# Queries and keys of a pair of heads split together on 128 rows: per-row scales from the pair's own tiles, operands put in place by transfers inside SBUF

## The chip, the cores and the metric

The kernel runs on one core of one Trainium2 chip. The metric is the device time of one execution in microseconds (us), the median of the runs shown. The core has a matrix engine (PE; PEld in the profile is its weight load), a vector engine (DVE), an activation engine (ACT), GpSimd (POOL), and SP, which here issues every transfer (DMA).

## The reference

Attention with a decay bias, and behind it a feed-forward layer on its output, all in fp32. B = 8 batches, H = 8 heads, S = 576 positions, head size 64; 4608 rows of 512 through a layer of 2048.

```python
scores = q @ k.T / sqrt(64)
cum = cumsum(max(s, 0));  bias = -(cum[:, None] - cum[None, :])
scores = where(causal, -1e6, scores + min(bias, 0))
attn = softmax(scores);  out = attn @ v
x = out.transpose(0, 2, 1, 3).reshape(4608, 512)
h = x @ w_in;  g = where(h > 0, h, exp(min(h, 0)) - 1)
result = g @ w_out
```

The weights come as 64-bit floats and are decoded to fp32 on the chip.

## The kernel before

**A plan orders everything.** The program lists its operations, each with a priority, the engines that could do it and a cost in ns for each (class Plan, from L86 on). The planner goes through them by the earliest possible start and then by priority, chooses the engine where there is a choice, and fixes each engine's order. On the chip each engine goes through its own order and waits where data is missing. So a change of one operation can move many others, on every engine. PE gets matmuls on a scratch bank (L1501) where the plan has nothing for it at the start.

**Pieces.** The work on attention goes by pairs of heads (four pairs a batch). First come the *low pairs*: the first 320 positions of batches 0 to 3, 16 pairs, computed with fp32 matmuls (prepare_low, scoring_low, weighing_low; tiles kl, ql, vs, products avl and trl). Then the *main pairs*: batches 4 to 7 whole (a short block of 64 positions of both heads, whose names carry None, and then each head with four blocks of 128 rows), and the late rows of batches 0 to 3 (each head with two blocks): 32 main pairs. A unit of these is prepared (prepare), scored (scoring: matmuls, a custom DVE step, L1053, exp on ACT, L1058), normalised, transposed by SP (L389, tiles T<-p, 192 times) and multiplied by the values (weighing, L1212).

The feed-forward layer goes by chunks of rows. The first chunk is *native*, in fp32 straight on the decoded weights (L1377 first layer, L1431 second). The 17 *main* chunks work on splits: every fp32 factor is scaled by a power of two, rounded to fp16 (the high part; `scaled`, whose ways are POOL L408, ACT L409, DVE L410), and the remainder is a second fp16 number. Three matmuls then stand for one (L1381, L1438).

**Weights.** load_unit brings a piece of a weight (tile raws), decodes it (ACT L675, DVE L679 and L684) and takes its peak (L606 on DVE or L609 on ACT). weight_scales (through scales_of: L629 on DVE, PE `flat` L640, DVE L632 to L636, PE `every` L643, DVE L645) makes the scales from all the peaks. Then split_unit makes the 32 high parts and the 32 remainders (DVE, L699), which the main chunks need. The scale of the low pairs' values is made in the same call, as its third span:

```python
scales_of(-600, [(A_IN, NF + 1), (A_OUT, NF + 1), (A_LOW, N_CUT * NP + 1)], 0)
```

A_LOW is the range of the peaks of V of all 16 low pairs. The first main chunk takes rows of low pairs, whose scales (chunk_scales, cs) come from this call.

**Main pairs.** For each of the 8 groups (a batch, or its late rows), group_values loads the values (va), loads all q and k of the group once more into tile sx (8 loads of 288 KB a group) and takes their peaks (128 rows by 1152, L606 or L609). From them come the group's scales of v, q and k. prepare then works head by head. K and Q lie in tiles stk and stq twice, on rows 0 to 63 and 64 to 127. The high parts are made on all 128 rows (kh, qs). The q high part on 64 rows goes to tile q2 by a transfer (L384 q<-qs). The remainders are taken on 64 rows (L1008): for q in the lower rows of qs, for k in the upper rows of k2. Below them stand three rows of decay (aux). A score is two matmuls per block (L1050): qs by kh, and q2 by k2.

Of the kernel before, what the change touches and what calls it, by code (L numbers as in the profile page):

```python
# [9 lines left out]
F32 = mybir.dt.float32  # L10
# [7 lines left out]
P = 128  # L18
# [9 lines left out]
N_ST, N_A, N_AV, N_H, N_IO, N_G, N_X, N_T, N_K, N_V = 3, 2, 1, 3, 3, 1, 1, 2, 2, 4  # L28
# [307 lines left out]
def kernel(  # L336
# [178 lines left out]
    def weigher(q):  # L515

        def rows():
            t = q.v[HB:]
# [7 lines left out]
        return rows  # L526

    def ones():

        for q, k in ((q2s, k2s), *zip(q2, k2)):  # L530
            op(60, [("Pool-M", 2600.0, weigher(q))], [], [(q, "ones")])
            op(60, [("Pool-M", 400.0, lambda k=k: pool.memset(k.v[HB:], 0.0))], [], [(k, "aux")])
# [46 lines left out]

    groups = [(b, False) for b in range(N_CUT, B)] + [(b, True) for b in range(N_CUT)]  # L580
    A_LOW, A_IN, A_OUT = 0, N_CUT * NP + 1, N_CUT * NP + 1 + NF + 1
    A_GROUP = A_OUT + NF + 1
    A_EACH, N_SCALES = NP + 1 + 3 + 3, 6
    peaks = plan.buf(const, [P, A_GROUP + len(groups) * A_EACH], F32, "peaks")

    all_tops = [plan.buf(const, [P, P], F32, f"tops_{m}") for m in range(2)]
    all_ones = plan.buf(const, [P, P], F32, "all_ones")
    scales = plan.buf(const, [P, 4 + N_SCALES * len(groups)], F32, "scales")
# [14 lines left out]
    def peak(prio, n, src, reads, at, axis=mybir.AxisListType.X, aside=None, also=()):  # L603

        col = slice(at, at + 1)
        ways = [("DVE-SB", 100 + 1.04 * n, lambda: dve.tensor_reduce(  # L606
            peaks.v[:, col], src(), axis, ALU.max, apply_absolute_value=True))]
        if aside is not None:
            ways.append(("ACT", 480 + n / 1.2, lambda: act.activation(  # L609
                aside(), src(), AF.Abs, accum_out=peaks.v[:, col])))  # L610
        op(prio, ways, reads, [(peaks, at), *also])
# [131 lines left out]
    def prepare_low(u):  # L743
# [23 lines left out]
        peak(prio, n_low * D, lambda: u.vs.v, [u.vs], A_LOW + b * NP + j, mybir.AxisListType.XY,  # L767
# [840 lines left out]
```

## Time and profile before

| | |
|---|---|
| runs | 1047.59, 1048.26 (median), 1049.46 us |
| profiled execution, whole | 1049.36 us |
| its span, first to last instruction | 1047.6 us |
| granted clock of the matrix engine | 0.996 |
| PE / DVE / ACT / POOL busy | 1014.1 / 854.6 / 696.6 / 309.2 us |
| transfers | 169.26 MB, mean 162 GB/s |

Busy time leaves out waiting. In a view of the stretches of the span, busy time stands beside the length of each stretch, and the granted clock (1.00 is full) beside it. In a line of the order of time, what stands in square brackets is the idle time ahead of the instruction and who ended it. A group's line gives busy time and the mean ns of one. Line numbers of before and after differ: L1050 is L1030 in the changed kernel, L1053 is L1033, L1381 is L1370, L1377 is L1366, L1431 is L1420, L699 is L695, L645 is L641.

### The profile page before, as it was taken

To read this page: it belongs to the slowest core of one execution; us is meant where nothing else is said; L and a number is where in the kernel's file an instruction comes from. 1 tells how busy PE (TensorE), PEld (TensorE's weight loads), DVE (VectorE), ACT (ScalarE), POOL (GpSimd) and SP (SyncE) were. 2 spreads that over 40 slices of the span, in tenths; PEclk is the share of its full clock that TensorE was granted. 3 is DMA by queue.
4 is the path that set the end of the run, shared out by engine and by line. 5 is a ranking of instruction groups with operands and counts; after the bars stand their busy time and mean duration, and the time that the engine had idled before them with its cause. 6 is when DMAs were issued, how large, how long until landed. Compare 5 with 4: busy or idle time off the path is not lost.

```text
span 1047.6 us, 22165 instructions
## 1 busy us (share of the span) xinstructions
PE 1014.1 (97%) x7354; PEld 696.8 (67%) x7354; DVE 854.6 (82%) x2222; ACT 696.6 (66%) x1568; POOL 309.2 (30%) x545
## 2 busy tenths in 40 slices
PE   8879998999999999999999999999999999999998
PEld 7656764666666666666666766666666676767665
DVE  7898656988888988989998999889888888876232
ACT  4788677766776765667777766676666666765343
POOL 6343114123353332335354434123421122210000
PEclk9999999999999999999999999999999999999999
DMA  8999856458889886688758866876785856664000
GB/s 250 251 263 277 250 150 180 129 127 180 188 205 189 171 205 135 147 142 209 158 141 168 215 150 145 175 180 161 156 180 140 154 140 137 145 121 102 6 21 21
DMA packets 289843, 169.26 MB, mean 162 GB/s; under 512 B 205856, under 2 KB 263424, under 8 KB 289728
## 3 DMA queue, kind: packets, MB, share of 16 engines
q1 hardware_dynamic: 289728, 167.84, 68.6%
q8 instruction: 58, 0.95, 0.4%
q14 instruction: 57, 0.47, 0.2%
HBM read 98.99 MB, written 19.24 MB: 113 GB/s over the span
## 4 chain that ended last, share of the span: by engine, by line
PE 50%; DVE 3%; DMA 2%; issue 1%; SPq 1%; POOL 0%; ACT 0%; DVEq 0%; POOLq 0%
PE o L1438 21%; PE h L1381 20%; PE sc L1050 4%; PE av L1212 4%; DVE p L1111 1%; DMA stk<-in_kT_dram 0%; DMA T<-p 0%; DVE h L1413 0%; DVE p L1053 0%; DMA stq_None<-in_qT_dram 0%; SPq L389 0%; DMA stq<-in_qT_dram 0%; DMA q<-qs 0%; DVE qs L1008 0%; DMA xc<-x_dram 0%
## 5 line engine op out<-in xcount | busy, mean ns | idle before, releaser
L1381 PE MATMUL h<-xh,wp 128*128 128x256 f16 x2176 | 397.6, 274 | 6.0 <-DVE wp L699 3.4
L1438 PE MATMUL o<-wp,gg 128*128 128x512 f16 x1632 | 393.8, 379 | 0.0
L1381 PEld LDWEIGHTS <-wp 128*128 128x128 f16 x3264 | 318.7, 98 | 74.5 <-DVE wp L699 5.3
L1381 PE MATMUL h<-xl,wp 128*128 128x256 f16 x1088 | 297.7, 274 | 0.9 <-DVE xl L1357 0.9
L1438 PEld LDWEIGHTS <-gg 128*128 128x128 f16 x1632 | 158.3, 98 | 143.4
L1058 ACT ACTIVATE p<-p,mn 128x192 f32<-128x192 f32 (+1 forms) x224 | 139.7, 624 | 43.7 <-DVE mn L1053 40.8
L1111 DVE SCALAR_TENSOR_TENSOR p<-p,sm,p 128x512 f16<-128x512 f32 (+3 forms) x233 | 149.0, 666 | 5.5 <-ACT p L1107 4.2
L1393 ACT ACTIVATE g<-h,cs 128x512 f32<-128x512 f32 x136 | 93.1, 684 | 90.5 <-PE h L1381 89.8
L1413 DVE SCALAR_TENSOR_TENSOR h<-g,cs,h 128x512 f32<-128x512 f32 x136 | 102.0, 750 | 52.7 <-ACT g L1400 51.4
L1417 ACT ACTIVATE gg<-h 128x512 f16<-128x512 f32 x133 | 78.8, 592 | 60.9 <-DVE h L1413 57.8
L1053 DVE CUSTOM_DVE_ANT_0 p<-sc,maskw 128x192 f32<-128x192 f32 (+1 forms) x224 | 106.0, 484 | 15.4 <-PE sc L1050 10.2
L1420 DVE SCALAR_TENSOR_TENSOR gg<-h,gg 128x512 f16<-128x512 f32 x136 | 93.2, 685 | 18.2 <-ACT gg L1417 17.2
L1103 POOL TENSOR_SCALAR p<-p,sm 128x64 f16<-128x64 f32 (+3 forms) x80 | 52.3, 659 | 144.5 <-DVE sm L1064 68.5
L1107 ACT ACTIVATE p<-p,sm 128x512 f16<-128x512 f32 (+3 forms) x128 | 72.4, 588 | 18.0 <-issue 6.9
L1050 PE MATMUL sc<-kh,qs 128*128 128x192 f16 (+2 forms) x256 | 75.8, 300 | 1.3 <-DVE mn L1053 0.7
L1050 PE MATMUL sc<-k,q 128*128 128x192 f16 (+2 forms) x256 | 75.5, 299 | 0.8 <-DMA q<-qs 0.7
L1212 PEld LDWEIGHTS <-v 128*64 128x64 f16 x896 | 45.4, 110 | 20.2 <-issue 9.8
L1212 PE MATMUL av<-T,v 128*64 128x256 f16 (+5 forms) x896 | 58.6, 280 | 0.2 <-DMA T<-p 0.2
L408 POOL TENSOR_SCALAR v<-va,scales 128x320 f16<-128x320 f32 x37 | 22.4, 611 | 109.4 <-PE av L1212 91.3
L408 POOL TENSOR_SCALAR qs<-stq,scales 128x256 f16<-128x256 f32 (+1 forms) x36 | 25.2, 701 | 91.3 <-PE sc L1050 80.9
L1008 DVE SCALAR_TENSOR_TENSOR k<-stk,scales,kh 64x576 f16<-64x576 f32 x61 | 49.9, 819 | 0.5
L1400 ACT ACTIVATE g<-g 128x512 f32<-128x512 f32 x77 | 48.4, 628 | 2.0
(189 smaller groups left out, 1441.8 us busy)
## 6 DMA issues: line engine op xcount, KB each, us to landing
stk<-in_kT_dram SPq DMA_DIRECT2D x64, 288.0 KB
va<-in_vb_dram SPq DMA_DIRECT2D x32, 320.0 KB
sx<-in_qT_dram SPq DMA_DIRECT2D x32, 288.0 KB
sx<-in_kT_dram SPq DMA_DIRECT2D x32, 288.0 KB
raws<-in_w_in_dram SPq DMA_DIRECT2D x16, 512.0 KB
raws<-in_w_out_dram SPq DMA_DIRECT2D x16, 512.0 KB
out_dram<-ost SPq DMA_DIRECT2D x32, 256.0 KB
stq<-in_qT_dram SPq DMA_DIRECT2D x32, 256.0 KB
```

Of the source, the lines that this page charges most:

```text
L1050: pe_.matmul(view(sc.v[:, :cw]), l, r, start=n == 0, stop=n == len(pairs) - 1)
L1053: op(prio, [("DVE", 84 + dve_p(cw), lambda i=i, sc=sc: dve.tensor_tensor_reduce(pt.v[:, i * cw : (i + 1) * cw], sc.v[:, :cw], mv(i * cw, c ...
L1058: op(prio, [("ACT", 480 + w / 1.2, lambda: act.activation(pt.v[:, :w], pt.v[:, :w], AF.Exp, bias=mn.v[:, n - 1 : n], scale=-1.0, accum_out ...
L1107: ("ACT", 295 + n / 1.2, lambda part=part: act.activation(part(t16, 0), own(part), AF.Copy, scale=sm.v[:, r])),
L1111: ("DVE-SB", dve_2(n), lambda part=part: dve.scalar_tensor_tensor(part(t16, 1), own(part), sm.v[:, r], part(t16, 0), ALU.mult, ALU.subtract)),
L1212: pe_.matmul(av.v[w.h * HB : (w.h + 1) * HB, dst], w.values.v[:, w.h, kb, v], part(w, kb, m), start=kb == 0 and m == 0 and v == 0, stop=kb ...
L1381: pe_.matmul(columns(k), weight_part(f, 0, part)[1]()[:, c * P : (c + 1) * P], xx.v[:, c], start=(c == 0 and m == 0), stop=(c == NCB - 1 a ...
L1393: op(side, [("ACT", act_c(W) + (0 if native else 90), lambda: act.activation(g.v, hp.v, AF.Exp, scale=1.0 if native else by(3)))], [hp] + ...
L1413: op(side, [("DVE", dve_p(W), lambda: dve.scalar_tensor_tensor(hp.v, g.v, by(2 if sign[0] else 1), hp.v, ALU.mult, ALU.max))], [g, cs], [hp])
L1417: ("ACT", act_c(W), lambda: act.activation(gg.v[:, 0], hp.v, AF.Copy, scale=2.0**-DOWN)),
L1420: op(side, [("DVE", dve_p(W), lambda: dve.scalar_tensor_tensor(gg.v[:, 1], hp.v, 2.0**-DOWN, gg.v[:, 0], ALU.mult, ALU.subtract))], [hp, ( ...
L1438: pe_.matmul(acc[i].v, gg.v[:, g, at], weight_part(f, 1, part)[1](), start=(f == 0 and m == 0), stop=(f == NF - 1 and m == 2),)
```

## The change

1. *Scales.* The loads and peaks of sx are gone. group_values makes the scale of the values only. The scale of q and k is taken for each pair and for each row of its 128 (row d of one head, row d of the other): peaks over the pair's own stk and stq, and four small DVE steps (powers). A row's scale of q and that of k cancel in the product.
2. *Low values.* Each of batches 0 to 3 gets a scale of its own for its low values, made when its fourth pair's peak is there. The weights' scales are made from the weights' peaks alone.
3. *Preparing.* A pair is prepared at once: one head's K on rows 0 to 63 and the other's on rows 64 to 127 (two loads), Q the same way (two or four loads), then the high parts and the remainders of K and Q on all 128 rows of both heads, the short block included. Twelve transfers of 64 rows, from SBUF to SBUF, bring the parts to the four operands of a *set*: Q1 (high, low), Q2 (high, weights of the decay rows), K1 (high, high), K2 (low, decay rows). One more transfer brings the decay rows.
4. *Places.* There are two sets, used by turns: one in a place of its own, one in the place of w_all[1], which the decoded weights hold until they are split. va stays in w_all[0].

```diff
-    A_LOW, A_IN, A_OUT = 0, N_CUT * NP + 1, N_CUT * NP + 1 + NF + 1
+    A_LOW, A_IN, A_OUT = 0, N_CUT * (NP + 1), N_CUT * (NP + 1) + NF + 1
...
-        scales_of(-600, [(A_IN, NF + 1), (A_OUT, NF + 1), (A_LOW, N_CUT * NP + 1)], 0)
+        scales_of(-600, [(A_IN, NF + 1), (A_OUT, NF + 1)], 0)
...
+        if j == NP - 1:
+            scales_of(-600, [(A_LOW + b * (NP + 1), NP + 1)], C_LOW + b)
...
-        home = w_parts[NG - 1] if at == 0 else w_all[(at - 1) % 2]
+        home = w_parts[NG - 1] if at == 0 else w_all[0]
...
-        for kind in range(2):
-            for c in range(2):
-                sx = plan.buf(sb, [P, 2 * S], F32, f"sx_{at}_{kind}_{c}", tag="sx")
...
-                    load(prio, dst, src, [], [(sx, m)], HB * 2 * S * 4)
-                peak(prio, 2 * S, lambda sx=sx: sx.v, [], first + NP + 1 + 3 * kind + c,
-                     aside=lambda sx=sx: sx.v, also=[sx])
-        scales_of(prio, [(first, NP + 1), (first + NP + 1, 3), (first + NP + 4, 3)], col)
+        scales_of(prio, [(first, NP + 1)], col)
...
-        load(prio, lambda: u.q2.v[:HB, :w], lambda: u.qs.v[:HB, :w], [(u.qs, 0)], [(u.q2, "q")], HB * w * 2)
...
-        remainder(w, lambda: u.qs.v[low, :w], lambda: sq.v[low, :w], lambda: u.qs.v[low, :w], 0, low,
-                  [(u.qs, 0)], [sq, (u.qs, 1)])
-        remainder(n, lambda: k_own(u.k2, top), lambda: k_view(st.v[top, :n]), lambda: k_own(u.kh, top), 1, top,
-                  [u.kh], [st, (u.k2, "kl")])
...
+    def prepare_pair(u, o):
...
+        for m, rows in enumerate(HALF):
+            load(prio, lambda m=m, rows=rows: sk.v[rows, :n], lambda m=m: kT[b, :HB, 2 * j + m, :n], [], [(sk, m)],
+                 HB * n * 4)
...
+        peak(prio, w, lambda: sq.v[:, :w], [sq], 0, aside=lambda: unread(w), dst=pk)
+        peak(prio, n, lambda: sk.v[:, :n], [sk], 1, aside=lambda: unread(n), dst=pk)
...
+        op(prio, [("DVE-SB", 350.0, powers)], [(pk, 0), (pk, 1)], [(pk, 2)])
...
+            scaled(prio, size, high, x, lambda: by(m), [src, (pk, 2)], [(t, 0)])
...
+                ("DVE-SB", dve_2(size), lambda: dve.scalar_tensor_tensor(
+                    low(), x(), by(m), high(), ALU.mult, ALU.subtract)),
...
+        split(1, n, kp, sk)
+        split(0, w, qp, sq)
...
+                load(prio, dst, lambda own=own: src.v[own, part, :size], [(src, part)], [(o, (label, h))], HB * size * 2)
...
+        spread(kp, 0, n, top, K1, "kh")
+        spread(kp, 0, n, low, K1, "kh2")
+        spread(qp, 0, w, top, Q1, "qh")
+        spread(qp, 0, w, top, Q2, "qh2")
...
+        spread(kp, 1, n, top, K2, "kl")
+        spread(qp, 1, w, low, Q1, "ql")
```

What this does to the order is seen on three engines. On PE before, at the end of the low pairs: `flat` and `every` are the two small matmuls of the weights' scales (the third column of `every` is the low values), sc_3_4_0 is the last score of the last low pair, o is the native chunk, h<-xh the first main matmul.

```order
L640 MATMUL flat_2034<-ident,tops_145 128x128
L849 MATMUL avl_2_1994<-tl_2_1988,vs_103 64x192 x2
L834 MATMUL trl_2_2_2043<-ident,p_84 128x128
L834 MATMUL trl_2_2_2043<-ident,pl_3_2_1832 128x128
L1431 MATMUL o_1_1385<-wa_1514,gg_7_1928 128x512
L643 MATMUL every_2048<-own_2038,all_ones 128x3
L849 MATMUL avl_2_1994<-tl_2_1988,vs_103 64x64 x2
L1050 MATMUL sc_3_4_0_2055<-kl_3_1717,ql_3_1836 128x320
L1381 LDWEIGHTS wp_2057
L1381 MATMUL h_0_2108<-xh,wp_2057 128x256
```

On PE now, at the first of the low pairs of the last batch (sc_0): the two small matmuls of the weights' scales.

```order
L1420 MATMUL o_0_1318<-wa_700,gg_2_1501 128x512
L636 MATMUL flat_1621<-ident,tops_145 128x128
L847 MATMUL avl_3_1596<-tl_3_1591,vs_122 64x256 x2
L832 MATMUL trl_3_1_1631<-ident,p_87 128x128
L832 MATMUL trl_3_1_1631<-ident,p_180 128x128
L832 MATMUL trl_3_1_1631<-ident,pl_2_3_1384 128x128
L832 MATMUL trl_3_1_1631<-ident,pl_2_3_1397 128x128
L1420 MATMUL o_0_1318<-wa_700,gg_2_1501 128x512
L639 MATMUL every_1643<-own_1626,all_ones 128x2
L847 MATMUL avl_3_1596<-tl_3_1591,vs_122 64x192 x2
L1030 MATMUL sc_0_3_0_1649<-kl_0_1236,ql_0_1299 128x320
```

They stand two columns wide among the native chunk, three low pairs and most of a fourth ahead of the end. The first main matmul now stands behind the last score of the second of the last batch's four low pairs; the rest of that pair and the other two follow among the main matmuls:

```order
L1420 MATMUL o_1_1409<-wa_1362,gg_7_1872 128x512
L847 MATMUL avl_0_1918<-tl_0_1893,vs_103 64x192 x2
L832 MATMUL trl_0_2_1950<-ident,p_84 128x128
L832 MATMUL trl_0_2_1950<-ident,pl_3_0_1512 128x128
L1030 MATMUL sc_1_4_0_1953<-kl_1_1303,ql_1_1542 128x320
L1370 LDWEIGHTS wp_1651
L1370 MATMUL h_0_1959<-xh,wp_1651 128x256
```

On DVE now, in the same place: L695 are the remainders of the weights, the ISA rows of L1033 the custom step of a low softmax, gg and g steps of the native chunk, xl the first main chunk's remainder.

```order
L695 SCALAR_TENSOR_TENSOR wp_1651<-wa_404,scales,wp_1651 128x512
L695 SCALAR_TENSOR_TENSOR wp_1695<-wa_700,scales,wp_1695 128x512 x6
L1393 TENSOR_SCALAR g_5_1785<-g_5_1785 128x512
L695 SCALAR_TENSOR_TENSOR wp_1695<-wa_700,scales,wp_1695 128x512
L1398 SCALAR_TENSOR_TENSOR gg_5_1796<-h_5_1758,g_5_1785 128x512
L695 SCALAR_TENSOR_TENSOR wp_1695<-wa_700,scales,wp_1695 128x512
L695 SCALAR_TENSOR_TENSOR wp_1731<-wa_1044,scales,wp_1731 128x512 x7
L1393 TENSOR_SCALAR g_6_1832<-g_6_1832 128x512
L695 SCALAR_TENSOR_TENSOR wp_1731<-wa_1044,scales,wp_1731 128x512
L1398 SCALAR_TENSOR_TENSOR gg_6_1842<-h_6_1800,g_6_1832 128x512
L695 SCALAR_TENSOR_TENSOR wp_1733<-wa_1362,scales,wp_1733 128x512 x6
```

The remainders stand nearly all in one block among the native chunk's steps; before, they began behind the last low softmax and were spread over the first main chunk. On SP now, in the middle of a batch (T_1_1 and T_2_0 are the transposes of the second pair's second head and the third pair's first head, kp and qp the split parts of the fourth pair):

```order
L389 DMA_TRANSPOSE T_1_1_0_4726<-p_5_1_1_0_3_4734 128x9x128
L384 DMA set_1806<-kp_3_None_4813 64x576 x4
L384 DMA set_1806<-qp_3_None_4819 64x576 x4
L384 DMA set_1806<-kp_3_None_4813 64x576 x2
L384 DMA set_1806<-qp_3_None_4819 64x576 x2
L384 DMA stk_0_None_4909<-in_kT_dram 64x576
L384 DMA x_dram<-x_1_None_4674 128x576
L384 DMA stk_0_None_4909<-in_kT_dram 64x576
L384 DMA stq_0_None_4928<-in_qT_dram 64x64
L384 DMA stq_0_None_4928<-in_qT_dram 64x4x128
```

All twelve transfers of a pair stand behind the transposes of the pair that used the same set before, and one pair ahead of their use. Before, two or three transfers of a pair's q stood there.

More of the change, by code (lines that the diff above doesn't have):

```diff
@@ L524, in rows @@
                 )
[L526 to L532, printed above, removed]
+        op(60, [("Pool-M", 5200.0, rows)], [], [(o, "weights")])
+        op(60, [("Pool-M", 800.0, lambda: pool.memset(o.v[HB:, K2], 0.0))], [], [(o, "aux")])
     def mask_tiles():
@@ new lines, in prepare_pair, with spread, dst @@
+        split(1, n, kp, sk)
+        split(0, w, qp, sq)
+        u.w, first = w, (S - w, S)
+        def spread(src, part, size, rows, m, label):
+            for h, own in enumerate(HALF):
+                def dst(h=h):
+                    if m in (K1, K2):
+                        return o.v[rows, m, h, :size]
+                    return o.v[rows, m].rearrange("p h t -> p (h t)")[:, first[h] : first[h] + size]
+                load(prio, dst, lambda own=own: src.v[own, part, :size], [(src, part)], [(o, (label, h))], HB * size * 2)
@@ new lines, in prepare @@
+    def prepare(u):
+        if u.h == 1 or (u.h == 0 and not u.blocks[0]):
+            return
+        turn = pairs_seen[0] % 2
+        pairs_seen[0] += 1
+        if len(pair_sets) == turn:
+            pair_sets.append(plan.buf(sb, [P, 4, 2, S], F16, "set_1", tag=w_all[1].key[1]))
+        if pairs_seen[0] <= 2:
+            weigh(pair_sets[turn])
+        u.set = pair_sets[turn]
+        prepare_pair(u, u.set)
+        if u.h is not None:
+            return
+        b, j, prio = u.b, u.j, u.prio
+        u.vs = plan.buf(sb, [P, 1, 2, D], F32R, f"vs_{u.tag}", tag="vs0")
+        v_src = lambda: vb[b, j, :, 0:1]
@@ L1128, in scoring @@
         prio = u.prio
-        used = [u.kh, u.k2, (u.qs, 0), (u.qs, 1), u.q2]
+        o = u.set
+        used = [(o, part) for part in (
+            "aux", "weights", *((part, h) for part in ("kh", "kh2", "qh", "qh2", "kl", "ql") for h in (0, 1)))]
         if u.h is None:
@@ L1266, in attention @@
                     pair = pair_values(u, *values)
-                u.values, u.back = pair, values[1] + 3
+                u.values, u.back = pair, values[1] + 1
                 if u.h == 0:
@@ L1271, in attention @@
             prepared(u)
+            if type(u) is Unit and not hasattr(u, "set"):
+                u.set, u.w = operands
+            if type(u) is Unit:
+                operands = u.set, u.w
             if was is Low and was is not type(u):
@@ L1313, in chunk_scales @@
         cols = tuple(sorted({
[L1314 removed]
+            4 + N_SCALES * groups.index((b, late)) if (b, late) in groups else C_LOW + b for b, late, *_ in rows}))
         if cols in by_columns:
```

167 lines of the change are left out of this document (63 added, 104 removed).

## The prediction

> **What bounds the kernel now.** I began with the page's table of busy time, then took the stretches of the span, because an average over this program hides two different regimes.
>
> ```profile
> PE 1014.1 (97%) x7354; PEld 696.8 (67%) x7354; DVE 854.6 (82%) x2222; ACT 696.6 (66%) x1568; POOL 309.2 (30%) x545
> ```
>
> The stretches, in the columns from and to, length, then busy time and instructions of PE, PEld, DVE, ACT and POOL, the granted clock, the DMA share and GB/s:
>
> ```profile
> 0.00:25.00 25.00, 20.30 (x151) 18.00 (x152) 19.56 (x44) 11.59 (x34) 17.53 (x51) 1.00 0.87 242
> 25.00:50.00 25.00, 22.71 (x165) 17.51 (x163) 22.59 (x71) 19.75 (x61) 9.17 (x21) 1.00 0.92 245
> 50.00:75.00 25.00, 17.59 (x107) 12.31 (x105) 23.31 (x79) 20.77 (x66) 11.52 (x23) 1.00 0.97 275
> 75.00:100.00 25.00, 22.90 (x131) 17.21 (x131) 22.61 (x74) 22.34 (x68) 10.81 (x26) 1.00 1.05 287
> 100.00:125.00 25.00, 25.00 (x120) 16.98 (x119) 15.34 (x37) 16.94 (x43) 1.97 (x8) 1.00 0.89 242
> 125.00:150.00 25.00, 25.00 (x134) 17.50 (x134) 16.32 (x50) 18.39 (x54) 4.39 (x12) 1.00 0.57 156
> 150.00:175.00 25.00, 23.33 (x120) 13.66 (x119) 14.02 (x56) 15.31 (x42) 3.91 (x11) 1.00 0.68 179
> 175.00:200.00 25.00, 18.52 (x118) 12.52 (x118) 24.48 (x42) 20.28 (x38) 12.62 (x14) 0.86 0.48 139
> 250.00:450.00 200.00, 199.26 (x1494) 135.40 (x1491) 174.19 (x448) 137.09 (x303) 71.14 (x112) 1.00 0.80 179
> 450.00:650.00 200.00, 197.36 (x1481) 134.59 (x1476) 181.99 (x493) 139.95 (x325) 88.14 (x137) 1.00 0.75 166
> ```
>
> From 250 us on PE is the bound: it stands still for 400 - 199.26 - 197.36 = 3.4 us in 400. The change leaves every score, value and MoE matmul as it was, so nothing can be won there beyond those few microseconds. What can be won lies ahead of 200 us. Up to 100 us DMA (0.87 to 1.05) and DVE (22.6 to 23.3 of 25) are full, and PE's share is flattered by filler matmuls on a scratch bank:
>
> ```profile
> L1501 PE MATMUL scratch<-ident x181: 272/273/421, 2.3 to 50.5; 128*128 128x128 f32 x181
> ```
>
> From 150 to 200 us PE stands still for 1.67 + 6.48 = 8.2 us, and in the last of these slices its clock is down to 0.86. That gap is where I look closest. PE there:
>
> ```profile
> 174.00 0.81 PE L1050 MATMUL sc<-kl,ql 128*128 128x320 f32 x2
> 177.15 0.27 PE L1381 MATMUL h<-xh,wp 128*128 128x256 f16 x1 [2.35 <-ACT xh L409]
> ...
> 180.55 0.61 PE L1381 MATMUL h<-xh,wp 128*128 128x256 f16 x2 [1.93 <-DVE wp L699]
> ...
> 185.43 0.42 PE L1381 MATMUL h<-xl,wp 128*128 128x256 f16 x1
> 185.64 0.43 PE L1381 MATMUL h<-xh,wp 128*128 128x256 f16 x2
> ...
> 190.08 0.39 PE L1381 MATMUL h<-xh,wp 128*128 128x256 f16 x2 [1.46 <-DVE wp L699]
> ```
>
> The last score of the last low pair starts at 174.00 us; then PE has nothing until the split weights come. From 180.55 to 185.64 matmuls follow one another at half the later rate (two take 0.61 us at 180.55 and 0.39 at 190.08, one 0.42 and 0.27: steps of 0.2 and 0.12). Why the weights come so late stands in DVE's order of time:
>
> ```profile
> 168.87 0.62 DVE L606 TENSOR_REDUCE peaks<-vs 128x1 f32<-128x448 f32 x1
> ...
> 169.67 0.32 DVE L629 TENSOR_REDUCE tops<-peaks 128x1 f32<-128x17 f32 x3
> ...
> 173.84 0.16 DVE L645 COPY scales<-every 128x3 f32<-128x3 f32 x1 [0.89 <-PE every L643]
> ...
> 177.32 2.07 DVE L1357 SCALAR_TENSOR_TENSOR xl<-xc,cs,xh 128x512 f16<-128x512 f32 x2
> 179.32 2.27 DVE L699 SCALAR_TENSOR_TENSOR wp<-wa,scales,wp 128x512 f16<-128x512 f32 x2
> ```
>
> The scales of the weights are taken (L629) in one step with the scale of the low pairs' values, so they wait for the peak of the last low pair's V at 168.87 us. The weights themselves were ready much earlier. Tile raws, on which they are decoded, has its last decode and its last peak on ACT here (the columns give first and last start):
>
> ```profile
> L684 DVE SCALAR_TENSOR_TENSOR wa<-raws x32: 652/686/815, 26.4 to 138.5; 128x512 uint32<-128x512 uint32 x32
> L609 ACT ACTIVATE raws<-wa x17: 659/675/722, 27.8 to 139.3; 128x512 f32<-128x512 f32 x17
> ```
>
> Some 30 us, 139.3 to 168.9, pass between weights that are ready and scales that are asked for. All that while DVE has 8 to 11 of 25 us free.
>
> **The change, part by part.** *Scales.* Low values get a scale per batch, so the weights' scales wait for the weights alone. By the order, they move ahead of the third of the last four low pairs, and the first main matmul to just behind the last score of the second of these. When is that? With no other effect, the last peak of 139.3 + 0.9 plus the same way as now from L629 to the scales (169.67 to 173.84, some 4 us) gives 144 us. It can be earlier, because the loads and peaks of tile sx go, and these fall into the full stretch:
>
> ```profile
> L384 SPq DMA_DIRECT2D sx<-in_qT_dram x12: 471/532/1003, 7.4 to 128.2; - x12
> L384 SPq DMA_DIRECT2D sx<-in_kT_dram x8: 474/500/633, 23.9 to 99.8; - x8
> L606 DVE TENSOR_REDUCE peaks<-sx x6: 1342/1347/1353, 33.8 to 125.8; 128x1 f32<-128x1152 f32 x6
> L609 ACT ACTIVATE sx<-sx x3: 1147/1148/1164, 14.6 to 112.9; 128x1152 f32<-128x1152 f32 x3
> ```
>
> By 140 us that is 20 loads of 288 KB, 5.8 MB, or 22 us at the 260 GB/s of those rows; and 6 x 1.35 = 8 us of DVE, 3 x 1.15 of ACT. If DMA sets the pace of the decodes, the scales come at 144 - 22 = 122; if neither, at 144. DVE is nearly as full as DMA, and by the order it now decodes more weights ahead of each low pair, which holds those back. I take the saving nearer DVE's 8 us than DMA's 22 and count 4 us for the shorter queue behind it: 144 - 8 - 4 = 132.
>
> *The splits.* In the changed order the 32 remainders of the weights stand in one block on DVE, ahead of the second low pair's next softmax (L1033), on whose bank PE's next score waits. How long is the block?
>
> ```profile
> L699 DVE SCALAR_TENSOR_TENSOR wp<-wa,scales,wp 128x512 f16<-128x512 f32 x32 | 25.7, 852 | 0.0
> L1420 DVE SCALAR_TENSOR_TENSOR gg<-h,gg 128x512 f16<-128x512 f32 x136 | 93.2, 685 | 18.2 <-ACT gg L1417 17.2
> ```
>
> 32 x 0.852 = 27 us, plus four gg (2.7), two xl (2.1) and about 30 small steps of some 0.16 us like L645's (5): 37 us; at the 2.27 / 2 = 1.14 us of the first two it would be 46. PE has cover beneath it, the rest of the native first chunk: 32 h and 22 o instructions, each two matmuls in the trace, whose steps come from
>
> ```profile
> 125.79 2.75 PE L1377 MATMUL h<-x,wa 128*128 128x256 f32 x12
> ...
> 133.12 1.45 PE L1431 MATMUL o<-wa,gg 128*128 128x512 f32 x3
> ```
>
> (2.75 - 0.38) / 11 = 0.215 us and (1.45 - 0.59) / 2 = 0.43 us, where 0.38 and 0.59 are the durations of one: 64 x 0.215 + 44 x 0.43 = 32.7 us, and some 4 us of low scores and values among it. So 37 us on both engines: the main matmuls start at about 132 + 37 = 169 instead of 180.55.
>
> *What is then still owed.* A bit over two low pairs, about 3.2 us each on PE by their columns at that spacing (an estimate): 7 us, which stand among main matmuls and so don't idle PE. So the main stream of the change is level with a start at 169 + 7 = 176. Before, it starts at 180.55, and by 190.08 it has lost half of 5.1 us to the slow clock and 1.5 us to the last wait: level with 180.55 + 2.5 + 1.5 = 184.6. The gain is 8.6 us. Against it go the four further small steps of scales (flat and every on PE, 0.3 us each): at most 2.4 us, which sit among idle PE; I count 0.6. That leaves 8 us.
>
> *Preparing a pair.* After 200 us the change trades remainders on 64 rows for ones on 128 rows of two heads, and sends the halves to their places with 12 transfers a pair. By the order 64 sx loads, 80 transfers of q and 48 aux loads are gone, 384 set transfers are new, and from the first transpose on SP holds 909 transfers instead of 688. On SP:
>
> ```profile
> L384 SPq DMA_DIRECT2D q<-qs x64: 467/476/1351, 191.0 to 937.4; - x64
> L389 SPq DMA_TRANSPOSE T<-p x192: 1197/1260/3217, 241.1 to 959.7; - x192
> ```
>
> 192 x 1.26 = 242 us of transposes and 717 x 0.48 = 344 us of others make 586 of the 719 us from 241 to 960, 82%; before 242 + 496 x 0.48 = 480, 67%. It isn't the bound, and the order has each set complete about one pair ahead (a pair is some 719 / 32 = 22 us), which hides the transfers. On DVE, ACT and POOL work is lost: a 64-row remainder costs as much as one on 128 rows, since time goes by columns.
>
> ```profile
> L1008 DVE SCALAR_TENSOR_TENSOR k<-stk,scales,kh 64x576 f16<-64x576 f32 x61 | 49.9, 819 | 0.5
> L409 ACT ACTIVATE kh<-stk,scales 128x576 f16<-128x576 f32 x33 | 25.3, 766 | 7.0 <-DMA stk<-in_kT_dram 5.0 <-PE sc L1050 1.5 <-issue 0.3
> ```
>
> Per pair one K remainder (0.8) and one K high part (0.77) go and as much for Q, against two peaks and four small steps. That helps engines which don't bound. I count nothing, with -3.4 us (all of PE's rest) and + several as its ends. If SP's slack is gone, the next thing late is T and with it PE's value matmuls.
>
> The new loads bring 64 rows each where one brought 128. A transfer q<-qs of 64 rows took this long in the chain of waits:
>
> ```profile
> 565.39 3.00 DMA q<-qs
> ```
>
> [...]
>
> Sum: 1049.36 (the span of 1047.6 and 1.76 around it) - 8 = 1041.4 for an execution as profiled. That one is 1.10 above the median of the runs shown (1048.26), so 1040.3 on the median's scale; I say 1040.
>
> **Rivals.** *The weights are not ready sooner* (0.16). If decodes end where they did, scales come at 144, the block ends at 181 and the stream is level with 188: 3.4 us lost, 1052. If they come at 137 to 140, nothing is left: 1045 to 1048. For it: decodes also wait on ACT (16.9 to 22.3 of 25) and not only on DMA. *DMA paces all* (0.14): scales at 122, block end 159, level with 166, so 18.6 gained, less what the native chunk holds PE: 1030; with PE's rest of 3.4 gone 1026. For it: DMA's 0.87 to 1.05. *SP's queue is late* (0.16): this ends on the slower side. Twelve transfers at 0.48 us are 5.7 us between one unit's transposes and the next, on an in-order queue that is 82% full and whose issues also wait for splits; whenever a set or T comes late, PE waits, and nothing before it is left to run. It decides once a pair loses over 8 / 32 = 0.25 us. At 1 us a pair it is 32 - 8 = 24 us, 1072; at half of that 1056. Against it: PE stood only 3.4 us in 400 and the planner fills with MoE matmuls. *The change doesn't do what it says* (0.02): the weights' scales come early, but PE's first main matmul is held by its x (xh, L409, at 177.15) as late as before: 1048.
>
> **How the numbers follow.** My forecast, scales at 127 to 136, has 0.52: 1034 to 1045, likeliest 1040. Its neighbours carry 0.14 on the fast side, 0.16 about no change or a little above, 0.16 on the queue. Eight in ten are held by 1027 to 1053: it leaves out the queue at more than half a microsecond a pair and the far end of the fast rival. About 0.2%, 2.1 us, is what a measurement can tell from no change. Faster by more: 0.50 + 0.14 + 0.02 = 0.66; within: 0.02 of the forecast, 0.09 of the first rival, 0.02 of the last: 0.13; slower: 0.05 + 0.16 = 0.21.
>
> **What would show it.** Right: the copy of the weights' scales (L641) at 127 to 136 instead of 173.84; the first main matmul (L1370) at 163 to 173, followed by no slice with a clock under 0.95; PE at 99% from 250 us as before. Wrong: that copy at 140 or later, PE waiting on DVE's p (L1033) for long behind the block of splits, PE stalls after 250 us released by a set, by T or by av, or SP with waits on its own queue. If DVE's remainders of the weights average over 1.1 us, the block is the bound and most of the gain is gone.

## The result, and the profile after

The changed kernel takes 1147.41 us (1143.94 to 1149.92) against 1048.86 us for the kernel before: ratio 1.094, 95% interval 1.090 to 1.097. The forecast was 1040 us. The profiled execution took 1148.63 us, with a span of 1146.8 us. The page of the kernel after:

```profile
PE 1052.6 (92%) x7358; PEld 709.5 (62%) x7358; DVE 824.0 (72%) x2273; ACT 675.9 (59%) x1568; POOL 245.9 (21%) x436
```

DVE, ACT and POOL have less to do, as the diff says. PE has the same matmuls and is busy for 38 us longer. The stretches of the span say where the time went (columns as before: from, to, length, busy time of PE, PEld, DVE, ACT, POOL, granted clock, DMA share, GB/s):

```profile
150.00:175.00 25.00, 23.08 (x90) 13.29 (x89) 19.87 (x40) 8.39 (x21) 11.89 (x10) 0.93 0.15 42
175.00:200.00 25.00, 24.78 (x173) 16.39 (x173) 17.84 (x78) 17.14 (x50) 3.54 (x9) 1.00 0.35 96
200.00:225.00 25.00, 22.56 (x150) 14.56 (x149) 15.93 (x48) 13.23 (x34) 1.90 (x4) 0.93 0.37 97
...
250.00:450.00 200.00, 176.80 (x1270) 116.53 (x1268) 148.69 (x424) 116.73 (x278) 39.11 (x68) 0.98 0.66 144
450.00:650.00 200.00, 185.21 (x1345) 123.76 (x1344) 158.44 (x454) 126.30 (x297) 54.90 (x85) 0.98 0.68 151
650.00:850.00 200.00, 179.48 (x1328) 120.41 (x1327) 149.51 (x406) 115.04 (x248) 37.78 (x59) 0.98 0.66 146
850.00:1050.00 200.00, 186.74 (x1428) 126.80 (x1425) 134.35 (x341) 106.30 (x213) 28.38 (x52) 0.99 0.54 115
```

The hole at 175 to 200 us is closed (24.78 busy of 25, before 18.52), but in the slices on either side PE stands still for 1.9 and 2.4 us, both at a clock of 0.93. From 250 us on, where PE had stood still for less than one part in a hundred, it now stands still for 23, 15, 21 and 13 us of each 200, and no other engine is near full. All DMA engines together are less loaded than before. What is left is SP, which these columns don't show. Its transfers, with minimum, median and maximum of an issue in ns, in the kernel after:

```profile
L384 SPq DMA_DIRECT2D set<-kp_None x96: 483/587/1777, 192.8 to 642.0; - x96
L384 SPq DMA_DIRECT2D set<-qp_None x96: 462/594/1677, 198.5 to 649.4; - x96
...
L384 SPq DMA_DIRECT2D stq_None<-in_qT_dram x64: 465/622/1614, 184.4 to 627.5; - x64
...
L384 SPq DMA_DIRECT2D stk_None<-in_kT_dram x32: 465/594/1415, 174.7 to 604.8; - x32
```

A set transfer of 64 rows holds SP for 0.59 us, and a stk load, now of 64 rows, for 0.59 where it was 0.41 with 128. Added up over the trace, SP issues for 766 us instead of 598; between the first and the last transpose it is 661 us of 794 (83%) instead of 487 of 719 (68%). With the short gaps between issues (under 0.15 us each, 56 us in all) SP needs 717 us there, which is all of the 719 that this stretch took before. Its longer pauses are 78 us, before 190.

How long an issue took also went with how closely it followed another. Of the set transfers, the 272 that came within 0.08 us of the transfer ahead took 0.594 us (median), the 22 that came after more than 0.3 us took 0.50. Before, only 4 of the 64 transfers q<-qs came so closely, and their median over all is 0.476.

How that reaches PE can be followed at one place. SP in order of time, kernel after:

```profile
246.84 1.18 SPq L384 DMA_DIRECT2D set<-kp_None  x2
248.48 1.10 SPq L384 DMA_DIRECT2D set<-qp_None  x2
249.68 0.54 SPq L384 DMA_DIRECT2D x_dram<-x_None  x1
```

The store of the attention's result x_None stands behind set transfers in SP's queue. DVE of the same kernel:

```profile
252.14 0.23 DVE L424 COPY x_None<-av_None 64x64 f32<-64x64 f32 x1 [2.35 <-DMA x_dram<-x_None]
...
253.94 0.08 DVE L1033 DVE_READ_ACCUMULATOR2_ANT mn<- 128x1 f32 x1
```

DVE waits 2.35 us for that store, because its next result goes into the same buffer, and the softmax step behind it (L1033) comes late. PE:

```profile
254.08 0.40 PE L1030 MATMUL sc<-set 128*128 128x288 f16 x2 [1.60 <-DVE mn L1033]
```

PE has its next score in order there, and waits 1.60 us for the bank that this softmax step frees. PE's waits, summed over the run, are mostly of this kind and for transposes:

```profile
PE sc L1030 <- DVE mn L1033: 31.8, 32, 3.2
PE av L1197 <- DMA T<-p: 24.0, 15, 3.1
```

Before, the first of these was 7.5 us:

```profile
PE sc L1050 <- DVE mn L1053: 7.5, 10, 2.3
```

From 250 to 950 us alone, the two are 25.3 and 20.0 us; before they are 0.7 and 0.2.

And a wait can cost more than its length. After the longest of them, PE runs at half rate (kernel after, PE in order of time):

```profile
535.18 0.54 PE L1030 MATMUL sc<-set 128*128 128x448 f16 x2 [3.16 <-DVE mn L1033]
...
535.99 0.27 PE L1370 MATMUL h<-xl,wp 128*128 128x256 f16 x1
536.10 0.50 PE L1370 MATMUL h<-xh,wp 128*128 128x256 f16 x2
536.40 0.42 PE L1370 MATMUL h<-xl,wp 128*128 128x256 f16 x1
...
539.28 0.42 PE L1370 MATMUL h<-xl,wp 128*128 128x256 f16 x1
539.49 0.46 PE L1370 MATMUL h<-xh,wp 128*128 128x256 f16 x2
539.79 0.27 PE L1370 MATMUL h<-xl,wp 128*128 128x256 f16 x1
```

3.16 us of waiting are followed, 1 us later, by about 3.4 us at half rate (0.42 us for a matmul that takes 0.27 on either side; the granted clock from 536.3 to 539.6 us is 0.50), which is 1.7 us more. Not every wait has this behind it: after the 1.60 us at 254.08 the matmuls go on at a granted clock of 1.00.

The share of each can be read from one long stretch. First the kernel before, then the kernel after:

```profile
250.00:950.00 700.00, 695.95 (x5323) 475.78 (x5321) 618.69 (x1584) 476.25 (x1028) 228.38 (x366) 1.00 0.74 164
```

```profile
250.00:950.00 700.00, 634.18 (x4644) 423.15 (x4641) 532.02 (x1484) 413.06 (x937) 149.42 (x243) 0.98 0.66 146
```

679 matmuls fewer, at 695.95 / 5323 = 0.131 us each, are 89 us of work not done in these 700 us. PE stood still for 65.8 instead of 4.1 us, which is 62 us of it. The other 27 us are matmuls that took 0.137 instead of 0.131 us each. The granted clock of 0.98 makes 700 x 0.02 = 14 us of these; what the last 13 are isn't broken down.

### The profile page after: what moved, and what is told of

Read it like the earlier page. It is cut to its first block, busy times and chain, and to the rows that moved or that the text cites. A ratio compares the mean times of both kernels' runs of the same rounds, so it can differ in the third digit from the quotient of the medians.

```text
span 1146.8 us, 22254 instructions
## 1 busy us (share of the span) xinstructions
PE 1052.6 (92%) x7358; PEld 709.5 (62%) x7358; DVE 824.0 (72%) x2273; ACT 675.9 (59%) x1568; POOL 245.9 (21%) x436
## 4 chain that ended last, share of the span: by engine, by line
PE 30%; DMA 10%; DVE 10%; SPq 6%; issue 5%; ACT 3%; POOL 1%; DVEq 0%; ACTq 0%; POOLq 0%
PE h L1370 14%; PE o L1427 13%; SPq L384 5%; DMA T<-p 4%; DMA stq<-in_qT_dram 2%; DVE p L1033 2%; PE sc L1030 2%; DVE p L1091 2%; PE av L1197 2%; DVE h L1402 2%; DMA va<-in_vb_dram 2%; DMA x_dram<-x_None 1%; SPq L389 1%; DMA stq_None<-in_qT_dram 1%; ACT p L1038 1%
## 5 line engine op out<-in xcount | busy, mean ns | idle before, releaser
L1370 PE MATMUL h<-xh,wp 128*128 128x256 f16 x2176 | 404.2, 275 | 0.6 <-DVE gg L1409 0.6
L1427 PE MATMUL o<-wp,gg 128*128 128x512 f16 x1632 | 398.2, 383 | 4.3 <-ACT gg L1406 2.7
L1030 PE MATMUL sc<-set 128*128 128x288 f16 (+3 forms) x512 | 108.0, 303 | 28.6 <-DVE mn L1033 28.1
L1033 DVE CUSTOM_DVE_ANT_0 p<-sc,maskw 128x192 f32<-128x192 f32 (+1 forms) x224 | 106.0, 483 | 13.0 <-PE sc L1030 9.5
L1087 ACT ACTIVATE p<-p,sm 128x512 f16<-128x512 f32 (+3 forms) x135 | 77.9, 594 | 51.7 <-DMA T<-p 32.6
L1083 POOL TENSOR_SCALAR p<-p,sm 128x512 f16<-128x512 f32 (+3 forms) x78 | 45.8, 592 | 239.3 <-DVE sm L1044 59.0
L1030 PEld LDWEIGHTS <-set 128*128 128x128 f16 x544 | 51.3, 99 | 73.5 <-issue 43.5
L1197 PE MATMUL av<-T,v 128*64 128x256 f16 (+5 forms) x896 | 66.9, 290 | 25.0 <-DMA T<-p 24.0
L1197 PEld LDWEIGHTS <-v 128*64 128x64 f16 x896 | 50.4, 114 | 48.0 <-issue 23.6
L1030 PE MATMUL sc<-kl,ql 128*128 128x192 f32 (+2 forms) x150 | 43.9, 393 | 5.2 <-DVE mn L1033 3.7
L1393 DVE TENSOR_SCALAR g<-g 128x512 f32<-128x512 f32 x72 | 31.2, 434 | 15.8 <-ACT g L1382 15.2
```

Of the source, the lines that this page charges most:

```text
L1030: pe_.matmul(view(sc.v[:, :cw]), l, r, start=n == 0, stop=n == len(pairs) - 1)
L1033: op(prio, [("DVE", 84 + dve_p(cw), lambda i=i, sc=sc: dve.tensor_tensor_reduce(pt.v[:, i * cw : (i + 1) * cw], sc.v[:, :cw], mv(i * cw, c ...
L1087: ("ACT", 295 + n / 1.2, lambda part=part: act.activation(part(t16, 0), own(part), AF.Copy, scale=sm.v[:, r])),
L1197: pe_.matmul(av.v[w.h * HB : (w.h + 1) * HB, dst], w.values.v[:, w.h, kb, v], part(w, kb, m), start=kb == 0 and m == 0 and v == 0, stop=kb ...
L1370: pe_.matmul(columns(k), weight_part(f, 0, part)[1]()[:, c * P : (c + 1) * P], xx.v[:, c], start=(c == 0 and m == 0), stop=(c == NCB - 1 a ...
L1427: pe_.matmul(acc[i].v, gg.v[:, g, at], weight_part(f, 1, part)[1](), start=(f == 0 and m == 0), stop=(f == NF - 1 and m == 2),)
```

## The experiments

The theory: SP's queue, which the twelve 64-row transfers a pair fill, makes everything behind it late. The rivals: the preparation of a pair in one go is itself too long a chain; or the order is merely planned on wrong costs, and a right one would lose nothing. Kernels without an interval were timed once, beside the kernel before on the same chip; between them a few microseconds tell nothing.

**The same load on the kernel before.** Nine transfers of 64 rows a main pair are added to the kernel before, from the constant mask tile to a spare DRAM tensor. Nothing else changes in what is computed.

```diff
...
+        if h is not None:
+            for k in range(5 - h):
+                load(prio, lambda k=k: spare.v[u.n, k], lambda: maskw.v[:HB, :448], [(u.qs, 0)], [(spare, (u.n, k))], HB * 448 * 2)
```

> The kernel before with nine further transfers of 64 rows a main pair on SP (288 in all, from a constant tile to a spare DRAM tensor, nothing waits for them): about the 174 us by which SP's issues grew between the first and the last transpose (487 to 661 us). Theory of the queue (SP's longer queue alone makes PE wait, however the operands are made): 1100 to 1160 us. Rival (the way a pair is prepared, peaks, powers, splits and two sets, is what is late, SP is only busy): under 1060 us.

It took 1119.68 us, 71 more than the 1048.75 of before. SP's rows of this kernel and its PE in the long stretch:

```profile
L384 SPq DMA_DIRECT2D spare<-maskw x288: 445/594/1867, 190.4 to 1014.8; - x144
```

```profile
250.00:950.00 700.00, 646.51 (x4771) 432.72 (x4769) 559.72 (x1442) 439.25 (x954) 201.84 (x320) 0.99 0.76 170
```

Nobody waits for these transfers, they only stand in SP's queue, and PE still loses 49 us by standing, at a clock of 0.99. The preparation is that of before. So load on the queue, without any change to the preparation, can cost most of what the change cost; the rival of the chain falls as the main cause.

**Their shape.** The same nine, of 128 rows by 224 instead of 64 by 448.

```diff
+    spare = plan.buf(dram, [96, 5, P, 224], BF16, "spare")
...
+                load(prio, lambda k=k: spare.v[u.n, k], lambda: maskw.v[:, :224], [(u.qs, 0)], [(spare, (u.n, k))], HB * 448 * 2)
```

> The nine idle transfers a pair once more, of the same 57 KB each and in the same planned order on every engine, but of 128 rows by 224 instead of 64 rows by 448. In the traces so far SP takes 0.33 to 0.43 us to issue a load of 128 rows and 0.47 to 0.62 us for 64 rows. If the time an issue takes on SP is what counts, an issue here takes about 0.40 us, SP is loaded 279 x 0.2 = 56 us less than with 64 rows, and the loss of 71 us falls to 30 to 50 us (1080 to 1100). If the number of transfers or their bytes count, it stays at 1110 to 1130 us.

It took 1094.30 us, 44 more than the 1050.53 of before. The order on every engine is planned alike and the bytes are the same; SP's issues differ:

```profile
L384 SPq DMA_DIRECT2D spare<-maskw x288: 319/432/1888, 194.6 to 989.3; - x144
```

0.43 instead of 0.59 us an issue, and a loss of 44 instead of 71. With number and bytes equal, 27 us go with the shape and the time that an issue of it holds SP. Whether the shape also changes something behind the issue, these two runs can't tell.

**Another queue.** The changed kernel with its set transfers issued by ACT.

```diff
-                load(prio, dst, lambda own=own: src.v[own, part, :size], [(src, part)], [(o, (label, h))], HB * size * 2)
+                op(prio, [("ACT", 600.0, lambda dst=dst, own=own: nc.scalar.dma_start(dst(), src.v[own, part, :size]), LAG,
+                           HB * size * 2)], [(src, part)], [(o, (label, h))])
```

> The changed kernel with its twelve set transfers a pair issued by ACT instead of SP, planned at 600 ns each. Theory of the queue: SP is relieved of 232 us and the loss goes for the greater part, 1040 to 1085 us, less so if ACT's own order then becomes late. Rival (the preparation's chain is late): over 1120 us.

1058.42 us, 10 more than before. ACT's issues and PE's long stretch:

```profile
L967 ACTq DMA_DIRECT2D set<-kp_None x96: 468/477/1342, 189.4 to 619.2; - x96
...
L967 ACTq DMA_DIRECT2D set<-qp x96: 468/524/1753, 633.2 to 938.9; - x96
```

```profile
250.00:950.00 700.00, 688.82 (x5240) 470.87 (x5237) 608.32 (x1658) 397.14 (x869) 202.52 (x319) 1.00 0.74 155
```

All that the change does to a pair is still there: peaks, powers, splits, two sets, twelve transfers of the same bytes. Taken off SP and planned at 600 ns, it leaves a tenth of the loss. The queue and the planned cost both differ here from the changed kernel; the same 600 ns with the transfers left on SP leave 46 us (e4_cost600, below), so the queue by itself is worth 36. With this SP's queue is shown as the main cause from both sides, by load added and by load taken away. Not separated is whether it is the issuing alone or also what happens to transfers of one queue once they are issued.

ACT's shorter issues went with their spacing: the 216 that came more than 0.3 us after the transfer ahead took 0.468 us (median), the 120 that came within 0.08 us took 0.610.

**Fewer transfers.** The q high part goes to Q1 and Q2 in one transfer, so ten a pair, all on SP.

```diff
...
-        spread(qp, 0, w, top, Q1, "qh")
-        spread(qp, 0, w, top, Q2, "qh2")
+        spread(qp, 0, w, top, (Q1, Q2), "qh")
...
```

> The changed kernel with ten set transfers a pair instead of twelve: the q high part goes to Q1 and Q2 in one transfer. Theory of the queue: if an issue still takes 0.6 us, SP has 64 x 0.6 = 38 us less, and the loss of 99 us falls in proportion to 174 us of further issues, by about 22 us: 1115 to 1135 us. If the transfer of two destinations takes twice the issue time, or the loss has another cause: 1140 to 1155 us.

1118.31 us, 68 over before (1050.53). A merged transfer takes 0.61 us, hardly more than a single one. SP's sum falls by 34 us and the loss by 31, more than in proportion. The merged transfers:

```profile
L384 SPq DMA_DIRECT2D set<-qp x64: 461/610/2060, 640.7 to 955.5; - x64
```

**What the plan is told.** Three kernels change only the cost in ns that the plan reckons for SP's transfers: the set transfers alone at 600 (e4_cost600), those, stk, stq and the transposes as measured (e9_true_costs), and the idle nine on the kernel before at 620 (f2_idle_told). Of each a line or two, in this order:

```diff
-                load(prio, dst, lambda own=own: src.v[own, part, :size], [(src, part)], [(o, (label, h))], HB * size * 2)
+                op(prio, [("SP", 600.0, lambda dst=dst, own=own: nc.sync.dma_start(dst(), src.v[own, part, :size]), LAG,
+                           HB * size * 2)], [(src, part)], [(o, (label, h))])
...
-                 HB * n * 4)
+                 HB * n * 4, cost=600.0)
...
-        op(prio, [("SP", 1250.0, lambda: nc.sync.dma_start_transpose(dst(), src()), LAG,
+        op(prio, [("SP", 1350.0, lambda: nc.sync.dma_start_transpose(dst(), src()), LAG,
...
+                load(prio, lambda k=k: spare.v[u.n, k], lambda: maskw.v[:HB, :448], [(u.qs, 0)], [(spare, (u.n, k))], HB * 448 * 2, cost=620.0)
```

> The changed kernel with the plan told that a set transfer takes SP 600 ns instead of 430 (the median of them in the trace is 0.59 us). If the loss comes from an order planned on too short a queue, the new order gets at least half of it back: 1060 to 1100 us. If SP's queue is late whatever the order, or the cause is another, it stays at 1130 to 1160 us.

> The changed kernel, all transfers still on SP, planned with the issue times that the traces show: set transfers and stk 600 ns, stq 640, transposes 1350. With the set transfers alone at 600 the loss was 46 us instead of 99. If what is left of it comes from what the plan still counts too low (the sum of SP's issues in the trace was 764 us against 695 planned), the loss falls below 25 us, 1050 to 1073. If a queue that is over 80% full is late whatever the order expects, it stays at 1085 to 1100.

> The kernel before with the nine idle transfers a pair of 64 rows again (1120 us), the plan told that each takes 620 ns instead of 430. Nobody waits for their data, so only SP's time counts. If the loss of 71 us comes mostly from an order planned on too short a queue, it falls to 15 to 35 us (1064 to 1084). If a queue that is 85% full is late in any order, it stays at 1100 to 1120.

1094.82 us (46 over before), 1080.78 us (31 over its 1049.46) and 1111.35 us (62 over 1049.55, instead of 71). With the same transfers on SP, 764 to 766 us of issues each, the changed kernel loses 99, 46 or 31 us by the order alone. So more than half of its loss was an order planned on issues that last longer than planned. The stretch from the first to the last transpose is 791 to 800 us in all three, against 719 before; what the order changes is how long PE stands still in it: 72, 37 or 25 us. But for the idle transfers the truth helps little, as their expectation has it for a queue that is late in any order, and 31 us stay in the best order that was tried with all transfers on SP. Neither alternative holds by itself.

**Both queues.** The plan may give each set transfer to SP (600 ns) or ACT (470 ns).

```diff
...
+                op(prio, [("SP", 600.0, lambda move=move: move(nc.sync), LAG, HB * size * 2),
+                          ("ACT", 470.0, lambda move=move: move(nc.scalar), LAG, HB * size * 2)],
...
```

> The changed kernel where the plan may give each set transfer to SP (600 ns) or to ACT (470 ns, as measured with all of them on ACT, which gave 1058 us). Theory of the queue: 1045 to 1065 us, as the plan leaves most on SP only where it has room; should it leave the half on SP, whose other 64-row loads it still plans at 430 ns, up to 1075.

1080.80 us, 30 over before: above the range expected. The plan left 221 of 384 on SP.

**One part alone.** The kernel before with the low values' scales taken apart from the weights'.

```diff
-        scales_of(-600, [(A_IN, NF + 1), (A_OUT, NF + 1), (A_LOW, N_CUT * NP + 1)], 0)
+        scales_of(-600, [(A_IN, NF + 1), (A_OUT, NF + 1)], 0)
...
+        if j == NP - 1:
+            scales_of(-600, [(A_LOW + b * (NP + 1), NP + 1)], C_LOW + b)
...
```

> The kernel before with one part of the change alone: a scale per batch for the low values, so that the weights' scales wait for the weights only. If the early part of the prediction's sum was right and the loss lies in the pairs' preparation, this kernel is about 8 us faster than before (1036 to 1044). If the early start of the splits is given back later anyway, it is level with before, within 2 us.

1051.89 us: 0.37% slower, interval 0.20 to 0.54%. The scales come earlier; DVE and PE of this kernel:

```profile
146.38 0.15 DVE L647 COPY scales<-every 128x2 f32<-128x2 f32 x1
```

```profile
171.75 0.27 PE L1385 MATMUL h<-xh,wp 128*128 128x256 f16 x1
```

Here the loads and peaks of sx stay, and the scales come close to the 144 us that the prediction gives for this part alone. The main matmuls start at 171.75 without a break instead of at 177 to 181 us with breaks, and nothing is won. PE's work done by a certain time says why, if each matmul is counted by its columns at the steps of the traces at a clock of 1.00 (0.11 us for 256 columns in fp16, 0.215 in fp32) and the fillers are left out (an estimate, good to a microsecond or two): by 100 us it is about 51 us instead of 59, by 175 us about 126 instead of 135, by 200 us about 150 in both. PE falls 8 us behind on the low pairs, and the closed gap returns just these.

Most of the 8 us are lost between 75 and 100 us, where PE stands still for 5.8 us instead of 2.1, mostly for low softmax steps, and its clock is 0.87 instead of 1.00. Earlier decodes of the weights don't explain it, for in this kernel the last decode starts at 141.0 us, before at 138.5. What in the new order does it stays open.

**The rest of 10 us.** Six kernels looked for it. Two of them change only the number of buffers of x, the changed kernel (e8_x_two) and the kernel before (f4_before_x2):

```diff
-N_ST, N_A, N_AV, N_H, N_IO, N_G, N_X, N_T, N_V = 3, 2, 1, 3, 3, 1, 1, 2, 4
+N_ST, N_A, N_AV, N_H, N_IO, N_G, N_X, N_T, N_V = 3, 2, 1, 3, 3, 1, 2, 2, 4
...
-N_ST, N_A, N_AV, N_H, N_IO, N_G, N_X, N_T, N_K, N_V = 3, 2, 1, 3, 3, 1, 1, 2, 2, 4
+N_ST, N_A, N_AV, N_H, N_IO, N_G, N_X, N_T, N_K, N_V = 3, 2, 1, 3, 3, 1, 2, 2, 2, 4
```

> The changed kernel with two buffers of the attention's result (tile x) instead of one. In the trace DVE waited 2.35 us at 249.8 us for the store of the buffer before, which SP had issued late behind set transfers; DVE's softmax and PE's scores stood behind it. If this wait carries the lateness of the queue to PE, a good part of the loss goes: 1085 to 1125 us. If the lateness reaches PE mainly through the transposes and the sets, it stays above 1130 us.

> The kernel before with two buffers of tile x. If the store of x holds it too: 1040 to 1045 us. If not, within 2 us of 1048.

The changed kernel took 1145.05 us with two buffers, the kernel before 1048.49 (ratio 0.999, 0.997 to 1.001): no change in either. PE's waits in the changed kernel with two buffers, beside 24.0 and 31.8 with one:

```profile
PE av L1197 <- DMA T<-p: 36.2, 21, 3.9
PE sc L1030 <- DVE mn L1033: 26.4, 20, 4.2
```

The waits for softmax steps fall from 31.8 to 26.4 us and those for transposes rise from 24.0 to 36.2. So the store of x was one way for the lateness to reach PE, and not the one that sets the time.

The other four have the sets on ACT. e10_act_ten has ten transfers a pair, planned at 500 ns, and SP's own loads at their measured times; e11_act_ten_low is the same with the low scales made with the weights' again; f1_act_low has twelve transfers and those low scales; f3_act_low_x2 adds two buffers of x to it.

```diff
+                op(prio, [("ACT", 500.0, move, LAG, n * HB * size * 2)], [(src, part)], [(o, (label, h))])
...
-        scales_of(-600, [(A_IN, NF + 1), (A_OUT, NF + 1)], 0)
+        scales_of(-600, [(A_IN, NF + 1), (A_OUT, NF + 1), (A_LOW, N_CUT * NP + 1)], 0)
```

> The changed kernel with ten set transfers a pair, all issued by ACT and planned at 500 ns, and SP's own loads and transposes planned at their measured times. Set transfers on ACT gave 1058. If the rest of 10 us is still lateness of the queues, 1045 to 1055; if it lies elsewhere (the early stage, more work in one go), 1055 to 1062.

> As the kernel before this one, and the scale of the low values made with those of the weights again, as before the change. That part alone cost the kernel before 0.4%. If it costs the same here: 3 to 4 us less than e10_act_ten, 1041 to 1052. If the early scales help here, it is slower than e10_act_ten.

> The changed kernel with its twelve set transfers a pair on ACT (planned at 600 ns, which gave 1058 us), and the scale of the low values made with those of the weights again. If the early scales cost what they cost alone on the kernel before (0.4%), 1052 to 1056 us; if the last 10 us lie in the pairs' preparation, 1057 to 1062.

> As f1_act_low, with two buffers of tile x. If the store of x holds DVE also when SP has room, 1044 to 1050 us; if not, the same as f1_act_low within 3 us.

They took 1076.50, 1064.76 (ratio 1.015, 1.013 to 1.018), 1064.32 (1.015, 1.012 to 1.017) and 1061.12 us. Ten transfers planned at 500 ns, with SP's own costs told, are worse than twelve planned at 600 ns, where ACT's issues in truth take 0.47 to 0.53 (medians by tile): a miss, and the cause isn't settled. The kernel with twelve transfers and the early scales taken back is above both of its ranges too. Taking the early scales back gains 12 us in the one pair of kernels and loses 6 in the other, so the expectation of 3 to 4 us is not borne out. What the last 10 to 15 us are stays open; from 250 to 950 us PE stands still for 11 us in the kernel with twelve on ACT against 4 before.

**The kernel before, told the truth.** Its transposes planned at 1350 ns, q transfers at 530, stq at 510, aux at 320.

```diff
...
-        op(prio, [("SP", 1250.0, lambda: nc.sync.dma_start_transpose(dst(), src()), LAG,
+        op(prio, [("SP", 1350.0, lambda: nc.sync.dma_start_transpose(dst(), src()), LAG,
...
```

> The kernel before, planned with its measured times on SP (transposes 1350 ns, q transfers 530, stq 510, aux 320). Its queue is two thirds full and PE stands still for 5 us between 250 and 950, so the theory of the queue gives no more than these back: 1044 to 1051 us. If the plan's costs matter by themselves, below 1040.

1049.97 us against 1049.46: nothing, as expected for a queue that has room. No kernel here is shown to beat the one before.

The runs side by side: SP's issues added up over the whole trace, and the time over the kernel before beside it (us).

| kernel | transfers on SP | SP issues for | loss |
|---|---|---|---|
| before | 907 | 598 | - |
| after | 1099 | 766 | 99 |
| after, plan told set costs | 1099 | 764 | 46 |
| after, plan told all costs | 1099 | 764 | 31 |
| after, ten transfers | 1035 | 732 | 68 |
| after, either queue | 936 | 672 | 30 |
| after, sets on ACT | 715 | 545 | 10 |
| before, idle nine of 64 rows | 1195 | 790 | 71 |
| before, the same, told | 1195 | 795 | 62 |
| before, idle nine of 128 rows | 1195 | 754 | 44 |

## Why the prediction was wrong

*The early stage, right in its steps, without its gain.* The kernel after, DVE:

```profile
130.09 0.16 DVE L641 COPY scales<-every 128x2 f32<-128x2 f32 x1 [0.63 <-PE every L639]
134.09 2.07 DVE L695 SCALAR_TENSOR_TENSOR wp<-wa,scales,wp 128x512 f16<-128x512 f32 x3
...
163.76 1.40 DVE L695 SCALAR_TENSOR_TENSOR wp<-wa,scales,wp 128x512 f16<-128x512 f32 x2
```

and its PE:

```profile
163.89 3.54 PE L1420 MATMUL o<-wa,gg 128*128 128x512 f32 x4 [1.92 <-DVE gg L1398]
...
173.92 0.27 PE L1370 MATMUL h<-xh,wp 128*128 128x256 f16 x1
```

The scales came at 130 (forecast 132), the block of splits ended at 165 (169), the main matmuls started at 174 (169). The block thus ended as forecast, but PE had more left ahead of the main matmuls. By the same estimate as above, PE had done about 126 us of work at 175 us where before it had done about 135, and by 200 us about 150 in both. So the term *what is then still owed* was too small: I set 7 us, it was about 9 to 11. Part of this PE lost at 162 us, where it waited 1.92 us for a step gg that stands in the block on DVE and then ran at half rate (four matmuls in 3.54 us; the granted clock from 164.2 to 167.6 us is 0.50). About 7 us had been lost ahead of 150 us. There the decodes do come earlier than before (the last starts at 123.0 instead of 138.5), and I had seen that they hold the low pairs back, and gave it no price; but the kernel with this part alone falls behind as far without earlier decodes, so they are not shown to be the reason. Of the 8.6 us, nothing remained. That the scales came when forecast is in part luck: without the sx loads and peaks they came 16 us earlier than in the kernel with this part alone, where I had taken 12, and whether DVE or DMA gave them isn't separated.

*Preparing a pair: the step that failed.* The prediction worked out SP's share at 82%, wrote that SP "isn't the bound", and counted nothing, because each set is complete one pair ahead. That the share came out at 83% is luck: the issues took 661 us instead of 586, and the stretch grew with them from 719 to 794. In the 719 us that the prediction divided by, 661 would have been 92%, and with the gaps between issues 717 us, so SP was full at the old pace. Two things were wrong in the step. The first is the inference: a queue in order need not be full all the time to make others late; this one issued for 83% of the stretch. What stands behind the set transfers is late by them too, stores of x and transposes among it, and these had no pair of slack; the chain at 246 to 254 us shows it, and the idle transfers show that it needs no consumer of the sets. The second is the price: I took the 64-row row q<-qs at 0.48 us for all transfers, and only 4 of its 64 issues closely followed another. The sets, stk and stq take 0.59 to 0.65 us, while the plan's order was built on 0.43. The kernel before was told nearly the truth by the same number (its stk of 128 rows: 0.41).

*The rival on the queue* was the right one, with its decisive point (0.25 us a pair) and its size at 1 us a pair. It came out three times as large: 99 us over 32 pairs are 3.1 us a pair. I held it at 0.16 because PE stood still for only 3.4 us in 400. That row spoke of a queue at two thirds. It says nothing of one at 83%. What the runs show behind the loss is SP's queue: an issue of 64 rows held it for 0.59 us, one of 128 rows and as many bytes for 0.43, and with the set transfers on ACT's queue, planned at 600 ns, the loss was 10 us instead of 99.

*The clock* was not in the sum of the late stage at all. About 14 of the 89 us between 250 and 950 us go by the granted clock of 0.98: it is 0.50 in seven stretches, six of 3.4 us and one of 6.8, each of them at a wait of PE of 2.4 to 3.2 us.

*The rivals of the early stage* (weights not ready sooner, DMA pacing all) played no part: the scales came when forecast.

## What to carry to other kernels

Before moving work from engines to transfers, add up what the issuing queue will hold, by the duration of issues of the same shape in the trace, and look at what stands behind them in that queue: here, what stood behind was late too. Kernels whose SP issued for 83 to 86% of the stretch lost 31 to 99 us, the one at 77% lost 30, those at 62 to 68% none to 27. Where an order is planned, the planned cost of a new kind of transfer must be its own, since an order built on too short a queue cost the changed kernel 53 to 68 of its 99 us (the idle transfers only 9 of 71). And a gap that closes in one place is won only if the stage ahead of it does not end as much later.

## What the runs showed of the hardware

- A transfer of 64 rows held the issuing queue longer than one of 128 rows of the same bytes: 0.594 us (e2_idle_nine) against 0.432 (e5_idle_wide) on SP (medians of 288 each, issued one close behind another). One with two destinations for the same 64 rows took 0.61 (e6_ten).
- The same set transfers took longer to issue when they closely followed another: 0.594 against 0.50 us on SP (after), 0.610 against 0.468 us on ACT (e3_act_queue).
- A wait of 3.16 us on the matrix engine was followed by 3.4 us at half its rate (granted clock 0.50, after), which cost 1.7 us more, about half of the wait again (an estimate from these); one of 1.60 us was not.
- A remainder on 64 rows took DVE about as long as one on 128 rows with as many columns: 0.819 us at 64 by 576 (before, L1008) against 0.81 to 0.89 at 128 by 576 (after, L950), and 0.535 against 0.527 us at 256 columns (means of each group).
